# Turning k and q on VectorE for seven more units, with two homes for the rows that are turned

## The chip, the cores and the metric

The kernel runs on one core of a Trainium2 chip. The metric is the device time of one execution in microseconds (us), the median of several runs. Beside the runs there is one execution taken by the hardware profiler; its span and its own time are given below.

## The reference

An mLSTM cell is followed by a multiplicative feed-forward block. The inputs q, k, v and o_gate have shape (4, 8, 768, 40): batch, heads, positions and head dimension, in float32. The weights of the feed-forward block are float64, w1 and w2 (320, 1024), w3 (1024, 1024), w_out (1024, 320).

```python
for t in range(S):                                   # the cell
    m_new = maximum(f[t] + m, i[t])
    f_stab, i_stab = exp(f[t] + m - m_new), exp(i[t] - m_new)
    m = m_new
    C = f_stab * C + i_stab * outer(v[t], k[t])
    n = f_stab * n + i_stab * k[t]
    h = C @ q[t];  denom = max(abs(n @ q[t]), 1)
    y[t] = sigmoid(o_gate[t]) * h / denom

x = y.transpose(0, 2, 1, 3).reshape(3072, 320)       # the feed-forward block
out = ((x @ w1) * (x @ w2)) @ w3 @ w_out
```

## The kernel before

**Units and steps.** The sequence is cut into 6 chunks of 128 positions, and each chunk of each of the 4 batches is a unit: 24 units, n from 0 to 23, each with all 8 heads. A unit is again two halves of 64 positions. The main loop runs over steps s from 0 to 29. In step s the function `quarter_work` computes the inner part of unit s (the products of k and q, `ss`, and the products that go into the state, `pc`) and the outputs of unit s - 1 (`ph`, `pi`), all in one PSUM tile named `cell`. Around it the step brings in the inputs of later units, does a part of the feed-forward block on tokens that are finished, and converts a piece or two of the weights.

**Turning.** The product of k and q needs both with the head dimension on the partitions. `turn(n)` makes `kT` and `qT` for a unit. Before the change it has two ways. For units below `N_DVE` = 17, TensorE transposes k and q from `kbuf` and `qbuf` by an identity, four 128x128 transposes each into a PSUM tile `pt`, and ScalarE copies each tile to SBUF; this is issued at the beginning of step n. For units from 17 on, `load_turned(n)` brings the rows of k and q from HBM in a layout of their own, eight loads of 80 KB in place of the load of q (k is loaded in the usual way too, as the state needs it), and VectorE transposes blocks of 32x32, one instruction for k and one for q; this is issued at the end of step n - 1, behind the last instruction of the outputs. The rows lie in `gates`, a memory whose first use, the recurrence over the gates, is over after the beginning. There is one home for them, so the rows of unit n + 1 can be written when those of unit n have been turned.

**The feed-forward block.** `x_trans` turns the cell's output of units 0 to 14 on TensorE (tile `px`); for later units it goes by way of HBM (`send`, `get_back`) and VectorE (`x_turn`). `up` and `up_rest` compute x @ w1 and x @ w2 into tiles `pa` and `pb`, ScalarE copies `pa` to `a_sb`, and VectorE multiplies `pb` by it into `ab`. `w3_mm` multiplies w3 by w_out once, block by block (tile `wp`), so that `ffn_out` needs one product (tile `po`). The tiles `pt`, `px`, `wp`, `pa`, `pb` and `po` take four PSUM banks in turn.

**Words.** The float64 weights come as raw 64-bit words. `fetch` calls a piece (512 KB, a tile `raw`, four buffers), ScalarE scales its upper words, and VectorE makes float32 of it in `to_f32` (four instructions, tiles `ex`, `ma`, then the result); a piece of w3 is also transposed on VectorE (`w3T`). Two or three pieces are converted in a step, two in each of steps 9 to 15. The number of pieces that are called ahead of those converted is two in the first two steps and three afterwards.

**What sets the order.** TensorE's instructions run in the order in which they are written (`in_order`). Up to step 6 the other engines keep the written order as well (`keep_order`). Afterwards the framework's planner orders them by its own estimates, within the dependencies; it may place a conversion of a step ahead of that step's `pw`. The outputs are held behind the product `pw` (`issue_after`). All loads and the writes to HBM inside the kernel are issued by SyncE, in one queue; only the final output and three loads at the start are issued by ScalarE. Each waits there until its buffer is free, and what stands behind it waits too. In the written order a step issues the broadcast weights `pw` of unit s + 3 (`load_u`), then k, q, v and the output gate of unit s + 2 (`load`, `load_o`), then the outputs' way through HBM (`send`), the turned rows of unit s + 1 (`load_turned`), `get_back`, and at the end the raw words.

Lines of the profile: matmuls are recorded at L90, transposes on TensorE at L93; L296 is ScalarE's copy of `pt`, L288 VectorE's transposes of the turned rows, L347 the product `pw`, L351 and L356 the state, L367 to L383 the outputs, L567 the eviction to `ab`; for SyncE, L125 loads k, q and v, L134 the turned rows, L139 the output gate, L145 `pw`, L170 the raw words.

Of the kernel before, what the change touches and what calls it, by code (L numbers as in the profile page):

```python
# [8 lines left out]
FP = mybir.dt.float32  # L9
# [7 lines left out]
def kernel(  # L17
# [28 lines left out]
    B, H, S, D = q.shape  # L46
    L = 64
    P = 128
    NT = S // L
    NT2 = S // P  # L50
    NU = NT2 * B
    NP = H // 2
    DP = 64
# [11 lines left out]
    const = ctx.enter_context(tc.tile_pool(name="const", bufs=1))  # L65
# [9 lines left out]
    def mps(shape, name):  # L75
        pool = banks.pop(0)
        banks.append(pool)
        return pool.tile(shape, FP, name=name, tag="m")
# [13 lines left out]
    def transpose(out, in_, n=P):  # L92
        in_order(nc.tensor.transpose(out, in_, ident[0:n, 0:n]))  # L93
# [4 lines left out]


    NB, NBQ = 4, 3  # L100
    N_DVE = 17
    qbuf = [const.tile([P, H, DP], FP, name=f"qbuf{i}") for i in range(NBQ)]
    kbuf = [const.tile([P, H, DP], FP, name=f"kbuf{i}") for i in range(NB)]
    vbuf = [const.tile([P, H, D1], FP, name=f"vbuf{i}") for i in range(NB)]
    ident = const.tile([P, P], FP, name="ident")
# [12 lines left out]
    def rows(src, n):  # L118
        c, b = divmod(n, B)
        return src[b, :, c * P:(c + 1) * P, :].rearrange("h p d -> p h d")  # L120

    def load(n):
        for dst, src in ((kbuf[n % NB][:, :, 0:D], k), (qbuf[n % NBQ][:, :, 0:D], q), (vbuf[n % NB][:, :, 0:D], v)):
            if src is not q or n < N_DVE:
                nc.sync.dma_start(out=dst, in_=rows(src, n))  # L125

    def load_turned(n):
        c, b = divmod(n, B)
        for dst, src in zip(turned_in, (k, q)):
            for hip in range(2):  # L130
                of = src[b].rearrange("(p two) s d -> two p s d", two=2)[hip, :, c * P:(c + 1) * P, :]
                for j in range(2):
                    p0, c0 = hip * DP + j * 32, (1 - j) * 32
                    nc.sync.dma_start(out=dst[p0:p0 + 32, c0:c0 + NP * RAW].rearrange("r (p e) -> r p e", p=NP),  # L134
                                      in_=of.rearrange("p (r f) d -> r p (f d)", f=4))

    def load_o(n):
        o_t[n] = io.tile([P, H, D], FP, name="o_in", tag="o_in", bufs=4)
        nc.sync.dma_start(out=o_t[n], in_=rows(o_gate, n))  # L139

    def load_u(n):
        c, b = divmod(n, B)
        src = U_d[2 * c:2 * c + 2, b * H:(b + 1) * H, :].rearrange("x h t -> x (h t)")
        for x in range(2):
            nc.sync.dma_start(out=weights_tile(n)[halves[x]].rearrange("p h t -> p (h t)"),  # L145
                              in_=src[x:x + 1].to_broadcast([L, H * L]))
# [76 lines left out]
    def scale_next():  # L223
        scaled.append(pend.pop(0))
        scale(scaled[-1][1])
# [31 lines left out]
    qT_t, kT_t, vw_t, before_t, y_t, x_t = {}, {}, {}, {}, {}, {}  # L257

    def out_gate(n):
        nc.scalar.activation(out=o_t[n], in_=o_t[n], func=AF.Tanh, scale=0.5)  # L260
# [11 lines left out]
    def weights(n):  # L272
        c, b = divmod(n, B)
        src = weights_tile(n) if c else spread(n)
        pw = weights_tile(n)
        for h in range(H):
            nc.scalar.activation(out=pw[:, h, :], in_=src[:, h, :], func=AF.Exp, bias=aT[:, c, b * H + h:b * H + h + 1])  # L277
        for r in halves:
            nc.gpsimd.affine_select(out=pw[r], in_=pw[r], compare_op=OP.is_ge, fill=0.0, base=0,  # L279
                                    pattern=[[0, H], [1, L]], channel_multiplier=-1)  # L280

    def turn(n):


        if n >= N_DVE:
            for src, dst, name in zip(turned_in, (kT_t, qT_t), ("kT", "qT")):
                dst[n] = sb.tile([128, NP, P], FP, name=name, tag=name)
                nc.vector.transpose(out=dst[n].rearrange("i p (r f) -> i p f r", f=4),  # L288
                                    in_=src[:, 32:TB].rearrange("i (p f d) -> i p f d", p=NP, f=4)[:, :, :, 0:32])
            return  # L290
        for src, dst, name in ((kbuf[n % NB], kT_t, "kT"), (qbuf[n % NBQ], qT_t, "qT")):
            pt = mps([128, NP, P], "pt")
            for p in range(NP):
                transpose(pt[:, p, :], src[:, 2 * p:2 * p + 2, :].rearrange("p a b -> p (a b)"))
            dst[n] = sb.tile([128, NP, P], FP, name=name, tag=name)
            nc.scalar.copy(out=dst[n], in_=pt)  # L296

    def weighted(n):
        c, b = divmod(n, B)
        vw_t[n] = sb.tile([P, H, D1], FP, name="vw", tag="vw")  # L300
        nc.gpsimd.tensor_tensor(out=vw_t[n], in0=vbuf[n % NB], op=OP.mult,
                                in1=wT[:, c, b * H:(b + 1) * H].unsqueeze(2).to_broadcast([P, H, D1]))

    def decayed(new, old, n, x):
        c, b = divmod(n, B)
        nc.gpsimd.tensor_tensor(out=new, in0=old, op=OP.mult, in1=decay[:, b * NP:(b + 1) * NP, 2 * c + x:2 * c + x + 1]  # L306
                                .to_broadcast([P, NP, D1]))
# [78 lines left out]
    def send(n):  # L386


        y = y_t.pop(n)
        for cc in range(KF):  # L390
            nc.sync.dma_start(out=y_d[n][:, :, cc, :], in_=y[:, cc * P:(cc + 1) * P].rearrange("t (i c) -> t i c", c=32))
        for i in range(0, 4, 2):
            nc.sync.dma_start(out=y_d[n][:, i:i + 2, KF, :], in_=y[:, KF * P:DM].rearrange("t (i c) -> t i c", c=32))
# [16 lines left out]
    def twice(n):  # L410
        nc.gpsimd.tensor_copy(out=y_t[n][:, DM:DM + REM], in_=y_t[n][:, KF * P:DM])
# [16 lines left out]
    TB = 32 + NP * RAW  # L428
    gates = const.tile([P, 2 * TB], FP, name="gates")
    f_sb, a, F, U, on = (gates[0:RG, i * TC:(i + 1) * TC] for i in range(5))  # L430

    turned_in = [gates[:, i * TB:(i + 1) * TB] for i in range(2)]
    w, g = f_sb, on
    M = const.tile([RG, GC + 1], FP, name="M")
    dec = const.tile([RG, GC], FP, name="dec")
# [151 lines left out]
    todo = w12[KF * 2 + 1:] + [("wo", i, 0) for i in range(FO)] + [("w3", ko, part) for ko in range(FO) for part in range(2)]  # L587
# [3 lines left out]
    turned, converted, fetched = 0, 2, 2 * KF + 1  # L591

    for s in range(len(n_up)):
        if B <= s + 3 < NU:
            load_u(s + 3)
        if s + 2 < NU:
            load(s + 2)
            load_o(s + 2)
        if 0 < s < B - 1:
            weights(s + 1)  # L600
            out_gate(s)
        if s < NU:
            weighted(s)
            if s >= B:
                decayed(state[s % B][1], state[s % B][0], s, 0)
            if 0 < s < N_DVE:
                turn(s)
        if NY <= s - 2 < NU:
            send(s - 2)
        elif 0 <= s - 2 < NY:  # L610
            twice(s - 2)
        if N_DVE <= s + 1 < NU:
            load_turned(s + 1)
        if NY <= s - 2 < NU:
            get_back(s - 2)
        while turned < min(s - 2, NY):
            x_trans(turned)
            turned += 1
        fold()
        for _ in range(n_down[s]):  # L620
            ffn_out(*downs.pop(0))
        now = [ups.pop(0) for _ in range(n_up[s])]
        open_ups = [up(*x) for x in now]
        if len(now) == 1 and turned == s - 2 < NY:
            x_trans(turned)
            turned += 1

        def rest():
            for x in open_ups:
                up_rest(*x)  # L630

        gated = None
        if s <= NU:
            gated = quarter_work(s, rest)
        else:
            rest()
        with tc.issue_after(gated.ins) if gated else nullcontext():
            if NY <= s - 2 < NU:
                x_turn(s - 2)
            if N_DVE <= s + 1 < NU:  # L640
                turn(s + 1)
        if s == 0:
            gate_cols(g, gT, nc.scalar.copy)
            out_gate(0)
            scale_next()
            weights(1)
        if s == NU:
            cell_psum.close()
            banks.append(ctx.enter_context(tc.tile_pool(name="ps_x", bufs=4, space=bass.MemoryType.PSUM)))
        if B - 1 <= s < NU:  # L650
            if s + 1 < NU:
                weights(s + 1)
            out_gate(s)
        for _ in range(n_cvt[s] if s < len(n_cvt) else 0):
            convert()
            converted += 1
        while todo and fetched < converted + (2 if s < 2 else 3):
            fetch(*todo.pop(0))
            fetched += 1
        if s + 1 == pinned:  # L660
            for ins in keep_order(front):
                behind.enter_context(tc.issue_after(ins))
# [30 lines left out]
```

## Time and profile before

| what | value |
|---|---|
| median of 3 runs | 474.29 us (473.12 to 476.47) |
| profiled execution, its own time | 475.94 us |
| profiled execution, span | 474.2 us |
| TensorE matmul busy | 450.0 us (95%) |
| VectorE busy | 241.0 us (51%) |
| ScalarE busy | 142.4 us (30%) |
| GpSimd busy | 84.2 us (18%) |
| moved by DMA | 49.28 MB in 135,770 packets, mean 104 GB/s |
| granted TensorE clock, mean | 0.986 |

The span reaches from the first instruction to the last; the execution's own time is 1.74 us longer. Busy times are shares of the span over stages that differ; matmuls overlap each other, so a busy TensorE need not be at its peak. PE is TensorE, PEld its weight load, DVE VectorE, ACT ScalarE, POOL GpSimd, and SPq SyncE's queue. A line of a timeline gives the start, the duration, the engine, the source line, the operation, what is written and read, the count, and in brackets how long the engine sat idle before it and what released it. The steps concerned start, by TensorE's transposes, at 106.55 us (step 9), 119.01 (step 10), 135.78 (11), 153.51 (12), 170.29 (13), 187.06 (14), 203.83 (15), 220.60 (16) and 237.37 (17).

### The profile page before, as it was taken

What the parts mean: (1) busy time and instruction counts of PE and PEld (TensorE: products, weight loads), DVE (VectorE), ACT (ScalarE), POOL (GpSimd) and SP (SyncE); (2) the same over time, 40 slices, a digit from 0 to 9 for tenths busy, and PEclk for the clock granted to TensorE, in tenths of its full rate; (3) what the DMA queues carried; (4) which work ended last, traced back from release to release, by engine and by line L of the source; (5) the groups of instructions that cost most, each with busy time, mean ns of one, the idle gap of its engine ahead of it and who ended that gap; (6) DMA issues with size and microseconds to landing.
All of it is one profiled execution on the core that took longest, in us unless ns stands there. A gap on an engine that the chain in (4) does not pass through costs nothing.

```text
span 474.2 us, 12856 instructions
## 1 busy us (share of the span) xinstructions
PE 450.0 (95%) x5375; PEld 362.3 (76%) x5375; DVE 241.0 (51%) x501; ACT 142.4 (30%) x390; POOL 84.2 (18%) x156
## 2 busy tenths in 40 slices
PE   2867999899999999999999999999999999999997
PEld 2766878788878888788878787787877778768864
DVE  6676698988865766785351523515236043111110
ACT  3643545544243263344331212211101111011111
POOL 5341333521220222213220211100000000000000
PEclk9995999999999999999999999999999999999999
DMA  7999978599987756432452546354240220200001
GB/s 174 181 166 173 214 138 157 118 201 194 185 165 111 167 104 149 85 65 55 82 121 61 122 105 136 58 127 88 61 116 11 53 43 20 62 14 15 1 15 41
DMA packets 135770, 49.28 MB, mean 104 GB/s; under 512 B 116320, under 2 KB 126752, under 8 KB 135712
## 3 DMA queue, kind: packets, MB, share of 16 engines
q1 hardware_dynamic: 132112, 44.42, 47.8%
q10 hardware_dynamic: 3600, 4.03, 2.5%
q8 instruction: 42, 0.69, 0.6%
q14 instruction: 16, 0.13, 0.1%
HBM read 42.63 MB, written 5.80 MB: 102 GB/s over the span
## 4 chain that ended last, share of the span: by engine, by line
PE 82%; DVE 7%; issue 7%; POOL 2%; ACT 1%; DMA 0%; SPq 0%; DVEq 0%; POOLq 0%
PE pa L90 23%; PE po L90 22%; PE pb L90 16%; PE cell L90 9%; PE wp L90 7%; PE pt L93 2%; DVE h L371 1%; PE ub L90 1%; ACT pw L277 1%; PE px L93 1%; DVE o_in L381 1%; POOL state L306 1%; DVE y L383 1%; DVE h L367 1%; DVE den L378 1%
## 5 line engine op out<-in xcount | busy, mean ns | idle before, releaser
L567 DVE TENSOR_TENSOR ab<-pb,a_sb 128x512 f32<-128x512 f32 x48 | 33.1, 691 | 159.8 <-ACT a_sb L566 159.6
L90 PE MATMUL po<-w3o,ab 128*128 128x320 f32 x384 | 106.2, 435 | 0.0
L90 PEld LDWEIGHTS po<-w3o,ab 128*128 128x128 f32 x384 | 72.1, 190 | 30.1 <-issue 0.4
L90 PE MATMUL pa<-xT,w 128*128 128x256 f32 x384 | 91.1, 380 | 0.6 <-ACT xT L421 0.6
L90 PE MATMUL pb<-xT,w 128*128 128x256 f32 x384 | 90.8, 379 | 0.0
L90 PEld LDWEIGHTS pa<-xT,w 128*128 128x128 f32 x384 | 72.3, 190 | 13.3 <-ACT xT L421 1.0
L90 PEld LDWEIGHTS pb<-xT,w 128*128 128x128 f32 x384 | 72.9, 190 | 10.2 <-ACT kT L296 0.3
L566 ACT ACTIVATE a_sb<-pa 128x512 f32<-128x512 f32 x48 | 28.6, 595 | 149.4 <-PE pb L90 149.4
L90 PE MATMUL pa<-xT,wr 64*64 64x256 f32 x384 | 47.0, 383 | 0.0
L90 PE MATMUL pb<-xT,wr 64*64 64x256 f32 x384 | 47.0, 383 | 0.0
L277 ACT ACTIVATE pw<-pw,aT 128x64 f32<-128x64 f32 x160 | 40.8, 338 | 18.1 <-DMA pw<-U_d 18.1
L279 POOL TENSOR_SCALAR_AFFINE_SELECT pw<-pw 64x512 f32<-64x512 f32 x48 | 35.8, 745 | 52.5 <-ACT pw L277 51.0
L306 POOL TENSOR_TENSOR state<-state,decay 128x164 f32<-128x164 f32 x40 | 19.5, 491 | 139.7 <-issue 53.6
L90 PEld LDWEIGHTS pa<-xT,wr 64*64 64x64 f32 x384 | 25.8, 132 | 16.8 <-issue 7.8
L90 PE MATMUL wp<-wo,w3T 128*128 128x320 f32 x128 | 35.8, 432 | 0.0
L574 ACT COPY o_sb<-po 128x320 f32<-128x320 f32 x24 | 10.2, 423 | 76.6 <-PE po L90 76.4
L90 PEld LDWEIGHTS cell<-vbuf,pw 64*64 64x64 f32 x768 | 27.7, 142 | 6.2 <-issue 2.0
L90 PEld LDWEIGHTS wp<-wo,w3T 128*128 128x128 f32 x128 | 23.7, 190 | 8.9
L90 PE MATMUL cell<-vbuf,pw 64*64 64x41 f32 x768 | 27.6, 232 | 2.4 <-issue 1.4
L347 DVE TENSOR_TENSOR pw<-cell,pw 128x512 f32<-128x512 f32 x24 | 16.5, 686 | 21.7 <-PE cell L90 21.7
L90 PEld LDWEIGHTS pb<-xT,wr 64*64 64x64 f32 x384 | 25.8, 132 | 0.0
L371 DVE TENSOR_TENSOR h<-cell,h 64x328 f32<-64x328 f32 x48 | 23.8, 497 | 1.1
(88 smaller groups left out, 463.4 us busy)
## 6 DMA issues: line engine op xcount, KB each, us to landing
raw<-in_moe_w_dram SPq DMA_DIRECT2D x64, 128.0 KB, 3.2
pw<-U_d SPq DMA_DIRECT2D x40, 128.0 KB, 4.1
kbuf<-in_k_dram SPq DMA_DIRECT2D x24, 160.0 KB, 4.6
vbuf<-in_v_dram SPq DMA_DIRECT2D x24, 160.0 KB, 5.0
o_in<-in_o_gate_dram SPq DMA_DIRECT2D x24, 160.0 KB, 3.7
out_dram<-o_sb ACTq DMA_DIRECT2D x24, 160.0 KB, 2.0
raw<-in_moe_w_dram SPq DMA_DIRECT2D x7, 512.0 KB, 6.0
qbuf<-in_q_dram SPq DMA_DIRECT2D x17, 160.0 KB, 5.0
```

The costliest lines, as they stand in the source:

```text
L90: in_order(nc.tensor.matmul(out, lhsT=lhsT, rhs=rhs, start=start, stop=stop))
L93: in_order(nc.tensor.transpose(out, in_, ident[0:n, 0:n]))
L277: nc.scalar.activation(out=pw[:, h, :], in_=src[:, h, :], func=AF.Exp, bias=aT[:, c, b * H + h:b * H + h + 1])
L279: nc.gpsimd.affine_select(out=pw[r], in_=pw[r], compare_op=OP.is_ge, fill=0.0, base=0, pattern=[[0, H], [1, L]], channel_multiplier=-1)
L306: nc.gpsimd.tensor_tensor(out=new, in0=old, op=OP.mult, in1=decay[:, b * NP:(b + 1) * NP, 2 * c + x:2 * c + x + 1] .to_broadcast([P, NP, D1]))
L347: first_read = nc.vector.tensor_tensor(out=pv, in0=ss, in1=pv, op=OP.mult)
L367: nc.vector.tensor_tensor(out=h.rearrange("p (n two) d -> p two n d", two=2), in0=pi, in1=gT[:, c, hs].rearrange("p (n two) -> p two n", t ...
L371: nc.vector.tensor_tensor(out=h[r], in0=ph[x], in1=h[r], op=OP.add)
L378: nc.vector.tensor_scalar(out=den, in0=den, scalar1=1.0, scalar2=2.0, op0=OP.max, op1=OP.mult)
L566: nc.scalar.mul(out=a_sb, in_=pa, mul=UP ** -2)
L567: nc.vector.tensor_tensor(out=ab_t[gr][j][:, fs[0]:fs[-1] + 1, t0:t0 + a_sb.shape[-1]], in0=pb, in1=a_sb, op=OP.mult)
L574: nc.scalar.copy(out=o_sb, in_=po)
```

## The change

`N_DVE` goes from 17 to 10: units 10 to 16 are turned by VectorE too, so their transposes on TensorE, ScalarE's copies and the plain loads of q go, and eight loads of turned rows and two transposes on VectorE come for each. The three buffers of q become slices of one memory, `q_all`. The turned rows have two homes that take turns: even units in `gates`, odd units in `q_all`, whose q rows are no longer needed by then. `load_turned(s + 1)` is issued as the first thing of step s, ahead of the loads of the units further on. From step 9 on (the tenth step), words are called two pieces ahead of the conversions where it was three.

```diff
     NB, NBQ = 4, 3
-    N_DVE = 17
-    qbuf = [const.tile([P, H, DP], FP, name=f"qbuf{i}") for i in range(NBQ)]
+    N_DVE = 10
+    q_all = const.tile([P, NBQ * H * DP], FP, name="q_all")
+    qbuf = [q_all[:, i * H * DP:(i + 1) * H * DP].rearrange("p (h d) -> p h d", d=DP) for i in range(NBQ)]
...
     def load_turned(n):
         c, b = divmod(n, B)
-        for dst, src in zip(turned_in, (k, q)):
+        for dst, src in zip(turned_in[n % 2], (k, q)):
...
         if n >= N_DVE:
-            for src, dst, name in zip(turned_in, (kT_t, qT_t), ("kT", "qT")):
+            for src, dst, name in zip(turned_in[n % 2], (kT_t, qT_t), ("kT", "qT")):
...
-    turned_in = [gates[:, i * TB:(i + 1) * TB] for i in range(2)]
+    turned_in = [[mem[:, i * TB:(i + 1) * TB] for i in range(2)] for mem in (gates, q_all)]
...
     for s in range(len(n_up)):
+        if N_DVE <= s + 1 < NU:
+            load_turned(s + 1)
         if B <= s + 3 < NU:
             load_u(s + 3)
...
             twice(s - 2)
-        if N_DVE <= s + 1 < NU:
-            load_turned(s + 1)
         if NY <= s - 2 < NU:
             get_back(s - 2)
...
-        while todo and fetched < converted + (2 if s < 2 else 3):
+        while todo and fetched < converted + (3 if 2 <= s < 9 else 2):
             fetch(*todo.pop(0))
```

## The prediction

> **What bounds the kernel now.** I read the page's busy line and its slices first, then the chain of waits in the steps concerned, then the busy time by step, then VectorE's and SyncE's timelines in one step. Busy line, and of the slices (11.9 us each) PE, DVE and DMA:
>
> ```profile
> PE 450.0 (95%) x5375; PEld 362.3 (76%) x5375; DVE 241.0 (51%) x501; ACT 142.4 (30%) x390; POOL 84.2 (18%) x156
> ...
> PE   2867999899999999999999999999999999999997
> DVE  6676698988865766785351523515236043111110
> DMA  7999978599987756432452546354240220200001
> ```
>
> TensorE is at 9 in all slices but one from the fifth to the last but one. What leaves its queue after 93 us shortens the run, unless another engine starts to hold it. But from 118 to 225 us (the 11th to the 19th slice), where the change works, DVE stands at 5 to 8, and DMA begins there at 9 and 8: the cover is thin.
>
> The chain of waits, around the last step with the old turning (16) and the first with the new (17); columns are start, us, what:
>
> ```profile
> 220.60 1.02 PE pt L93 x8
> 221.62 0.33 PE px L93 x3
> 221.95 4.31 PE wp L90 x16
> ...
> 235.05 2.32 PE cell L90 x123
> 237.37 0.48 PE px L93 x3
> 237.85 4.31 PE wp L90 x16
> ```
>
> The eight `pt` transposes of a unit lie on the path. From the end of `cell` to the start of `wp` it is 1.35 us with them (1.02 + 0.33) and 0.48 without.
>
> Busy time by step (columns: window, length, PE, PEld, DVE, ACT, POOL, clock, DMA share, GB/s), steps 10, 11, 13 and 16:
>
> ```profile
> 119.01:135.78 16.77, 16.77 (x221) 13.81 (x221) 12.25 (x26) 5.91 (x15) 2.73 (x6) 1.00 0.98 175
> 135.78:153.51 17.73, 16.98 (x221) 13.79 (x221) 11.54 (x24) 6.75 (x20) 3.91 (x6) 1.00 0.72 138
> ...
> 170.29:187.06 16.77, 16.77 (x220) 13.81 (x221) 11.88 (x25) 6.57 (x18) 4.78 (x9) 1.00 0.71 149
> ...
> 220.60:237.37 16.77, 16.77 (x220) 13.81 (x221) 8.65 (x18) 7.71 (x24) 5.47 (x9) 1.00 0.49 95
> ```
>
> A step is 16.77 us of TensorE work without a hole; step 11 has one of 0.76 us amid its `pt` (the chain calls it "issue"). VectorE has 4 to 8 us free.
>
> VectorE's timeline: where it idles in step 13, and what a turning costs it in step 17:
>
> ```profile
> 173.28 0.33 DVE L356 TENSOR_TENSOR state<-cell,state 128x164 f32<-128x164 f32 x1 [1.45 <-POOL state L306]
> ...
> 184.56 0.69 DVE L567 TENSOR_TENSOR ab<-pb,a_sb 128x512 f32<-128x512 f32 x1 [1.76 <-ACT a_sb L566]
> 185.75 0.69 DVE L567 TENSOR_TENSOR ab<-pb,a_sb 128x512 f32<-128x512 f32 x1 [0.50 <-ACT a_sb L566]
> 187.14 0.69 DVE L347 TENSOR_TENSOR pw<-cell,pw 128x512 f32<-128x512 f32 x1 [0.70 <-PE cell L90]
> ...
> 242.35 1.12 DVE L288 STREAM_TRANSPOSE kT<-gates 128x512 f32<-128x512 f32 x1
> 243.30 1.10 DVE L288 STREAM_TRANSPOSE qT<-gates 128x512 f32<-128x512 f32 x1
> ```
>
> SyncE's timeline at steps 9 and 10:
>
> ```profile
> 116.62 1.09 SPq L145 DMA_DIRECT2D pw<-U_d  x2
> 117.75 0.59 SPq L125 DMA_DIRECT2D kbuf<-in_k_dram  x1
> 118.38 0.58 SPq L125 DMA_DIRECT2D qbuf<-in_q_dram  x1
> 119.06 2.22 SPq L125 DMA_DIRECT2D vbuf<-in_v_dram  x1
> 121.38 1.01 SPq L139 DMA_DIRECT2D o_in<-in_o_gate_dram  x1
> 122.50 5.36 SPq L170 DMA_DIRECT2D raw<-in_moe_w_dram  x8
> ```
>
> SyncE has no hole here. It comes to step 9's loads at 116.6, when TensorE has been in step 9 since 106.55: ten us late. In steps 13 and 14 it is on time (172.15 and 185.68).
>
> **What the Trainium skill says.** "TensorE: Matmul & The Clock Gate", PE-mode transpose, gives about 275 ns for a 128x128 transpose inside a kernel. The trace agrees on one (median 273), but on the path they are pipelined, 1.02 / 8 = 0.13 us each. "VectorE: DVE Perf Modes", The three transpose paths: VectorE turns blocks of 32x32 only. That is why rows must be brought in a special layout; here one 128x512 takes 1.09. "Perfetto Trace Analysis", What "DMA-bound" means, names the issuing engine's sequencer, solid with DMA slices, as a bound of its own: SyncE looks so until about 145. "DMA: Bandwidth & Descriptors", Why small descriptors are slow: each packet pays about 3 beats over its 32-byte beats. The turned rows go in packets of 640 bytes (23 beats) where plain rows have 160 (8 beats), so by that page's figures, as an estimate, the four times as many bytes of a turned load of k and q against one plain load cost 2.9 times as much. No run so far isolates it.
>
> **The change part by part.**
>
> *TensorE.* Units 10 to 16 lose eight transposes each, seven steps times 1.35 - 0.48 = 0.87: 6.1 us off the path. The bounds: nothing, if another engine holds each step at 16.77; 10.4 us, if the mean busy time of the `pt` matmuls (25.2 us over 136, 0.185 each) were paid 56 times. I take 6.1, because step 17 shows the sequence without `pt`. The hole in step 11 (17.73 - 16.77 = 0.96) lies amid the removed work, but with "issue" as its cause it may reopen elsewhere: I take half, 0.5, between 0 and 1.0.
>
> *ScalarE* loses 14 copies of 0.59 us, 8.3 us. It is 30% busy and nothing waits for it there: worth nothing. PSUM tiles per step go from eight to six, so `px` and `wp` next take the banks of the first `pa` and `pb`. `wp` then waits for the first `ab` of the step before. In step 13 that ends at 185.25 and `wp` follows 0.48 after the cell's end at 187.06: some 2 us to spare.
>
> *VectorE* gains 14 transposes of 1.09, 2.18 per step. Steps 10 to 16 hold 78.6 us of it (the windows' DVE sum); with 15.3 more, 93.9 in a stretch of 118.4 - 7.1 = 111.3, or 84%. The fullest step is the tenth: 12.25 + 2.18 = 14.43, and its wait for GpSimd's `state` (1.05) makes 15.5 against a step of 15.90. In step 13, idle was 1.45 + 1.76 + 0.50 + 0.70 = 4.41; it must now hold 2.18 more in a step 0.87 shorter, so 1.36 is left, all inside the GpSimd wait. That wait shrinks when VectorE is late (0.58 at 238.96). So it fits, with about 0.4 to 1 us. Queued behind the transposes are the word conversions and the `ab` evictions, and for `ab` waits the bank of `wp`. I charge 0.5 us in all for a late eviction, between 0 and 6.1.
>
> *SyncE and DMA.* Per unit the plain q load goes (160 KB, 0.58 us of SyncE) and eight loads of 80 KB come (0.43 each where DMA is free, 0.67 as `raw` at 122.50 where it is full: 3.4 to 5.4 us). They now stand ahead of `pw`, k, v, `o_in` and the `y` writes of their step, and all of these go out that much later. A step's issues then come to 1.09 + 0.59 + 2.2 + 1.0 + 5.4 (`raw`) + 5.4 = 15.7 at most, against 15.9. In step 9 just one piece of words is called instead of two, since the lead drops from three to two: 512 KB and 2.7 us less, against 480 KB more of rows. So SyncE begins step 9 at about 116.0, the rows of unit 10 are out by 119.5 to 121.4 and land some 2.4 us later or a little more. VectorE's `y` of that step ended at 124.55, and `kT` is first in line. That is just in time. Unit 11: out by about 134.4, due after 139. Later ones keep some 3 us.
>
> The `pw`, k and v moved back are used one to two steps on. A piece called in step s is converted in step s + 1, and its buffer (four) held a piece converted in step s - 1, so SyncE no longer waits for `ma` in the same step (16.1 us of such waits after 140). I count that as nothing, since it lies off the path.
>
> *Two homes.* The rows of n go where those of n - 2 were, turned a whole step before. The first use of the new home overwrites q of units 8 and 9, read by 107.6; SyncE comes there at about 128. In steps 17 to 23 the loads merely go earlier; TensorE has no hole there: nothing.
>
> Sum: 6.1 + 0.5 - 0.5 = 6.1 us. The profiled execution took 475.94 with a span of 474.2; it becomes 469.8 with 468.1. The median of the runs is 1.65 under the profiled one: 474.29 - 6.1 = 468.2.
>
> **The rivals.**
>
> A. VectorE becomes the bound in steps 10 to 15. For it: 15.5 of 15.9, and an order in which conversions already slip ahead of `pw` (four of them ran at 134.75 to 137.9, and `pw` 2 us late). Against: step 8 ran 11.08 in 12.46 (89%) without a hole on TensorE. At 16.5 a step the gain is 7 x 0.27 = 1.9: 472.4.
>
> B. The rows come late, the slower end. SyncE at 15.7 a step and ten us behind doesn't catch up; VectorE, in order, stands before `kT`, with the conversions and `ab` behind it. Its step is 14.5 + 0.6 + the lateness; above 16.77 the change loses, so lateness over 1.7 us in each of the seven steps decides. At 3 us: 7 x 1.3 = 9.3 slower, 483.6. Against: step 10 already drops to 175 GB/s and SyncE has recovered by step 13, with waits of its own to give up.
>
> C. The q buffers, now slices of one memory, are held as one: each turning on TensorE in steps 1 to 8 would wait for the q load just issued (5.0 us to land). 8 x 5.0 is the most; with half of it 474.3 - 6.1 + 20 = 488. Against: in `gates`, sliced likewise, VectorE's memset ran at 0.9 us while a load into another slice landed at 2.7.
>
> D. The path pays the full 10.4: 463.9.
>
> **How the numbers follow.** About 1% (469.55 to 479.03) is what a measurement of this kernel can tell from no change. Main forecast 62%: 55 below 469.55, 7 within. A 18%: 2 faster, 16 within. B 12%: 10 slower, 2 within. C 5% slower. D 3% faster. That gives 0.60, 0.25, 0.15. The main case alone runs from 466.3 (no stall, the hole gone, 0.9 us for the runs' scatter) to 470.5 (2 us of late evictions); the range 465.8 to 476 takes in A, and leaves out D, C and most of B.
>
> **What would show it.** Right: no `pt` after 109 us; 15.9 us steps from 10 to 16 with `px` (0.48) straight after `cell`; step 17 starting some 6 to 7 us before 237.4; 12 to 14.5 us of DVE a step; landing of the turned rows before `y` ends. Wrong by A: PE waiting for `ab` at `wp` or `pa`. Wrong by B: DVE idle before `kT`, released by a DMA. Wrong by C: steps 1 to 8 longer, `pt` waiting for `qbuf`.

## The result, and the profile after

The changed kernel takes 512.24 us (511.29 to 513.13, four runs) against 475.38 in the same comparison: 1.0776 times as long, 95% interval 1.0715 to 1.0837. The prediction was 468.2 with a range to 476. It was wrong in sign and size.

The profiled execution took 513.13 with a span of 511.4. Of its page, the busy line, then TensorE's slices (12.8 us each here) and its granted clock:

```profile
PE 462.5 (90%) x5319; PEld 369.4 (72%) x5319; DVE 256.1 (50%) x515; ACT 135.0 (26%) x376; POOL 85.3 (17%) x156
...
PE   3888999899699786969687999999999999999997
...
PEclk9665899999979988889897999999999999999999
```

The work moved as meant: 56 transposes fewer on TensorE (5375 instructions became 5319), 14 more on VectorE. But TensorE has 12.5 us more of busy time, not less, it falls to 6 in four slices between 128 and 256 us where it stood at 9 before, and its clock falls with it. Busy time by step in the changed kernel (steps 10 to 16, columns as before):

```profile
120.95:142.83 21.88, 16.54 (x212) 13.42 (x213) 16.77 (x31) 5.75 (x15) 4.37 (x8) 0.93 0.87 182
142.83:160.65 17.82, 17.82 (x213) 14.16 (x213) 10.38 (x20) 4.71 (x14) 2.19 (x5) 0.89 0.73 158
160.65:181.38 20.73, 16.31 (x213) 13.18 (x213) 13.44 (x25) 5.64 (x16) 4.88 (x8) 0.99 0.45 111
181.38:203.78 22.40, 17.97 (x212) 14.38 (x213) 13.42 (x25) 5.39 (x15) 3.98 (x6) 0.88 0.47 113
203.78:226.91 23.13, 18.70 (x212) 14.76 (x213) 13.42 (x25) 5.39 (x15) 3.98 (x6) 0.87 0.46 104
226.91:250.43 23.52, 19.09 (x213) 15.02 (x213) 13.43 (x25) 5.38 (x15) 3.98 (x6) 0.86 0.32 65
250.43:272.43 22.00, 17.58 (x213) 14.16 (x213) 13.42 (x25) 5.40 (x15) 3.98 (x6) 0.89 0.32 65
```

The seven steps take 151.5 us; before they took 118.4. In six of them TensorE has a hole of 4.4 or 5.3 us (length less PE busy: 21.88 - 16.54, 20.73 - 16.31 and so on), 27.5 in all. The list of waits, for TensorE after 93 us, has the same sum and names the releaser:

```profile
PE cell L90 <- DVE qT L289: 27.5, 6, 5.3
```

TensorE waits in the middle of `cell`, at the products of k and q, for VectorE's transposed q. VectorE's timeline in step 10 shows why it is late:

```profile
126.22 0.47 DVE L384 TENSOR_TENSOR y<-h,o_in 128x320 f32<-128x320 f32 x1
...
131.49 0.71 DVE L239 STREAM_TRANSPOSE w3T<-w 128x512 f32<-128x512 f32 x1
134.34 0.69 DVE L568 TENSOR_TENSOR ab<-pb,a_sb 128x512 f32<-128x512 f32 x1 [2.14 <-ACT a_sb L567]
135.21 0.69 DVE L568 TENSOR_TENSOR ab<-pb,a_sb 128x512 f32<-128x512 f32 x1 [0.17 <-ACT a_sb L567]
135.81 0.42 DVE L187 TENSOR_SCALAR ex<-raw 128x512 uint32<-128x512 uint32 x1
...
139.06 0.71 DVE L239 STREAM_TRANSPOSE w3T<-w 128x512 f32<-128x512 f32 x1
139.70 1.04 DVE L289 STREAM_TRANSPOSE kT<-gates 128x512 f32<-128x512 f32 x1
140.59 1.06 DVE L289 STREAM_TRANSPOSE qT<-gates 128x512 f32<-128x512 f32 x1
142.90 0.69 DVE L348 TENSOR_TENSOR pw<-cell,pw 128x512 f32<-128x512 f32 x1 [1.26 <-PE cell L90]
```

Between the outputs (`y`, done at 126.7) and the transposes (139.7) stand three conversions (the third is a conversion of step 10 that was moved ahead) and both evictions of the next step, one of them at the price of an idle 2.1 us. The transposes are the last thing before `pw`, which needs their result. The rows of this unit had been there long before. SyncE's timeline:

```profile
117.08 1.87 SPq L135 DMA_DIRECT2D gates<-in_k_dram  x4
118.99 1.86 SPq L135 DMA_DIRECT2D gates<-in_q_dram  x4
```

The last load goes out by 120.85, and these eight loads land 2.5 to 3.6 us after issue (median 3.1), so by about 124.5, before `y` is done. VectorE stands idle before none of the transposes of these steps, but it idles earlier in the step, for other inputs. Step 13:

```profile
185.92 0.49 DVE L384 TENSOR_TENSOR y<-h,o_in 128x320 f32<-128x320 f32 x1
188.66 0.43 DVE L187 TENSOR_SCALAR ex<-raw 128x512 uint32<-128x512 uint32 x1 [2.25 <-ACT raw L176]
...
196.20 0.69 DVE L568 TENSOR_TENSOR ab<-pb,a_sb 128x512 f32<-128x512 f32 x1 [4.45 <-ACT a_sb L567]
...
200.65 1.04 DVE L289 STREAM_TRANSPOSE kT<-q_all 128x512 f32<-128x512 f32 x1
```

The rows of this unit went out by 162.94 and landed within 3.9 us, so both transposes could have run at 186.4. VectorE idles 6.7 us for other inputs and turns the rows 14 us later. It is the order in which the planner put them.

The rest of the loss is slower work, at a lower clock. From the chain of waits, `wp` in step 11, after a hole, and in step 12, with none before it:

```profile
143.66 5.88 PE wp L90 x16
...
161.13 4.31 PE wp L90 x16
```

The same 16 matmuls take 1.6 us longer after the hole. In the seven steps TensorE is busy for 124.0 us (the column's sum). That the hole causes this is tested below.

### The profile page after: what moved, and what is told of

Its sections match the earlier page's. It is cut to its first block, busy times and chain, and to the rows that moved or that the text cites. A ratio compares the mean times of both kernels' runs of the same rounds, so it can differ in the third digit from the quotient of the medians.

```text
span 511.4 us, 12828 instructions
## 1 busy us (share of the span) xinstructions
PE 462.5 (90%) x5319; PEld 369.4 (72%) x5319; DVE 256.1 (50%) x515; ACT 135.0 (26%) x376; POOL 85.3 (17%) x156
## 4 chain that ended last, share of the span: by engine, by line
PE 71%; DVE 10%; issue 9%; DMA 4%; POOL 2%; SPq 2%; ACT 1%; DVEq 0%; POOLq 0%; ACTq 0%
PE po L90 21%; PE pa L90 20%; PE pb L90 14%; PE wp L90 8%; PE cell L90 6%; DMA raw<-in_moe_w_dram 2%; DMA w3o<-in_moe_w_dram 2%; PE px L93 1%; DVE kT L289 1%; DVE qT L289 1%; DVE h L372 1%; POOL pw L280 1%; DVE ma L188 1%; DVE ex L187 1%; SPq L126 1%
## 5 line engine op out<-in xcount | busy, mean ns | idle before, releaser
L90 PE MATMUL pa<-xT,w 128*128 128x256 f32 x384 | 92.9, 386 | 0.6 <-ACT xT L422 0.6
L90 PEld LDWEIGHTS pa<-xT,w 128*128 128x128 f32 x384 | 73.4, 193 | 13.7 <-ACT xT L422 1.0
L307 POOL TENSOR_TENSOR state<-state,decay 128x164 f32<-128x164 f32 x40 | 21.0, 529 | 171.8 <-PE cell L90 79.4
L90 PE MATMUL cell<-qT,kT 40*64 40x64 f32 x768 | 22.1, 257 | 29.3 <-DVE qT L289 27.5
L280 POOL TENSOR_SCALAR_AFFINE_SELECT pw<-pw 64x512 f32<-64x512 f32 x48 | 35.8, 745 | 60.2 <-ACT pw L278 58.5
L90 PE MATMUL wp<-wo,w3T 128*128 128x320 f32 x128 | 45.0, 516 | 0.0
L90 PEld LDWEIGHTS cell<-qT,kT 40*64 40x64 f32 x768 | 18.3, 162 | 30.4 <-DVE qT L289 28.2
L90 PEld LDWEIGHTS wp<-wo,w3T 128*128 128x128 f32 x128 | 29.6, 238 | 12.8 <-issue 6.5
L575 ACT COPY o_sb<-po 128x320 f32<-128x320 f32 x24 | 10.2, 426 | 101.2 <-PE po L90 101.2
```

Of the source, the lines that this page charges most:

```text
L90: in_order(nc.tensor.matmul(out, lhsT=lhsT, rhs=rhs, start=start, stop=stop))
L575: nc.scalar.copy(out=o_sb, in_=po)
```

## The experiments

Three theories. 1: the order, as read above. 2: the rows land late (rival B). 3: VectorE has no room for 2.1 us more a step (rival A). Ratios are to the kernel before on the same chip.

**The transposes held in front.**

```diff
         def rest():
-            for x in open_ups:
-                up_rest(*x)
+            with after_turn(s):
+                for x in open_ups:
+                    up_rest(*x)
...
         for _ in range(n_cvt[s] if s < len(n_cvt) else 0):
-            convert()
+            with after_turn(s + 1):
+                convert()
```

`after_turn(n)` holds what VectorE does inside it behind the transposes of unit n.

> The changed kernel, with VectorE's order held by hand in steps 9 to 15: the two transposes of the turned rows come straight after the outputs, the word conversions of the step and the next step's ab evictions behind them. Nothing else differs. Theory 1 (order: the rows are there, but the planner put the transposes behind both conversions and both evictions, so that TensorE waits for qT in the middle of cell): no wait of PE for qT, steps 10 to 16 near 15.9 us, 467 to 470 in all. Theory 2 (the rows land late, rival B of the prediction): VectorE stands before kT, released by a DMA, with all else behind it; 500 or more. Theory 3 (VectorE has no room for the 2.1 us): steps of 17 us or more, 478 to 490.

525.24 us, ratio 1.1037 (1.0941 to 1.1133): slower than the change itself. Theories 1 and 3 miss. The number lies in the range of theory 2 (500 or more), but not by its mechanism: VectorE starts `kT` at 125.42, straight behind `y`, and waits for no rows. The wait for `qT` is gone and another has its place. TensorE's timeline in step 11 of this run:

```profile
135.79 0.55 PE L93 MATMUL px<-ident,y 128*128 128x128 f32 x3
143.19 7.09 PE L90 MATMUL wp<-wo,w3T 128*128 128x320 f32 x16 [6.85 <-DVE den L382]
```

`wp` waits 6.9 us. The name `den` is of what ran at the same moment; what `wp` reads is `w3T`, and VectorE's timeline has its second half finished at 143.04. With the transposes held in front, the planner put the conversions behind the evictions, where VectorE idled 5.7 us for `a_sb`, and the second conversion in among the next outputs. So theory 2 is out for this step; theories 1 and 3 were still open, for this run moved the order fault instead of removing it.

**The loads at their old place.** `load_turned(s + 1)` goes back behind the outputs' writes.

> The changed kernel, with the loads of the turned rows issued where they were before, behind the loads of the units further on and the writes of the outputs. Here the planner puts both conversions ahead of the evictions and the transposes behind them, so nothing but the two transposes (2.1 us) stands between the last eviction and the products of k and q. Theory 1 (order): TensorE waits some 2.2 us a step instead of 5.4, and keeps more of its clock: 480 to 490. Theory 2 (late rows): the loads go out later than in the changed kernel, so it is slower than 512. Theory 3 (no room): the same VectorE work as in the changed kernel, about 512.

488.48, ratio 1.0255 (1.0156 to 1.0355), and TensorE waits 12.8 us for `qT`, six times, instead of 27.5. Theory 1 had 480 to 490; theory 2 wanted it slower than the change, theory 3 about the same. Later loads made it 24 us faster: in steps 12 to 16 the planner now puts both conversions ahead of the evictions, and the wait is 1.5 us a step. In step 10 it still leaves a conversion between the evictions and the transposes, and there the wait is 5.3 as before.

**Three pieces ahead to the end.** The last hunk of the change undone.

> The changed kernel, with words called three pieces ahead to the end, as before. Theory 1 (order): the transposes stand last in VectorE's order in nearly all of steps 9 to 14 as well, so 503 to 514. If the shorter lead were the cause (words arrive late, conversions late, transposes behind them): well below, 475 or less. Theory 2 (late rows): one more piece of words ahead of the rows in SyncE's queue, so at or above 512.

512.06, ratio 1.075 (1.0649 to 1.0851), with 27.5 us of waits for `qT`. The shorter lead is not the cause. Between theories 1 and 2 this run doesn't decide, as it fits both.

**All but the seven units.** `N_DVE` back to 17, the rest of the change kept. In this run the second home is written while q rows are still wanted there, so a part of q is replaced by other rows; the work is the same.

> The changed kernel, with VectorE turning from unit 17 on as before; what remains of the change is the two homes, q as slices of one memory, the earlier place of the loads and the shorter lead of the words. Theory 1 (order) and theory 3: 473 to 477, since no transposes fall in steps 9 to 15. If the one memory or the shorter lead costs time by itself (rival C): longer steps 1 to 8 or 9 to 15, above 480.

478.13, ratio 1.0013 (0.9972 to 1.0054); 1.1 us more than expected, but no change against the kernel before. The one memory for q, the place of the loads and the lead cost nothing that shows, and rival C falls.

**The whole order held.** Beside the transposes, `pw` is held behind the evictions, the evictions behind both conversions, and ScalarE's `a_sb` behind its scaling of the words:

```diff
-            first_read = nc.vector.tensor_tensor(out=pv, in0=ss, in1=pv, op=OP.mult)
+            with tc.issue_after(done_ab[0].ins) if N_DVE <= n <= 16 else nullcontext():
+                first_read = nc.vector.tensor_tensor(out=pv, in0=ss, in1=pv, op=OP.mult)
...
         def rest():
-            for x in open_ups:
-                up_rest(*x)
+            with ExitStack() as es:
+                if N_DVE <= s <= 16:
+                    for ins in done.values():
+                        es.enter_context(tc.issue_after(ins.ins))
+                for x in open_ups:
+                    up_rest(*x)
...
-            convert()
+            with after_turn(s + 1):
+                convert()
```

`done` holds VectorE's last conversion and ScalarE's last scaling, `done_ab` the last eviction.

> The changed kernel, with VectorE's order of steps 9 to 15 held throughout: outputs, the two transposes of the turned rows, both conversions, the two evictions of the next step, then the product pw; ScalarE scales the words ahead of the next step's a_sb. The run pinned held only the transposes, and the planner pushed the conversions behind the evictions and in among the next outputs, where wp then waited for w3T. Theory 1 (order alone; the DMAs are in time and VectorE has room): no wait of PE for qT or w3T, steps 10 to 16 near 15.9 us, 467 to 471. Theory 2 (rows or words land late): VectorE stands before kT or ex, released by a DMA or by ScalarE's scaling, and the evictions behind it are late: 480 or more. Theory 3 (no room): VectorE without idle time, wp or pb waiting for ab: 475 to 485.

470.6, ratio 0.9869 (0.9827 to 0.9911), as theory 1 had it: 1.3% faster than the kernel before. Same instructions and loads as in the changed kernel, 42 us less. VectorE waits for no load between 93 and 250 us, so theory 2 is out for all these steps. Busy time by step, the first three and the last of the seven:

```profile
123.37:139.27 15.90, 15.90 (x213) 12.96 (x213) 13.22 (x26) 4.93 (x13) 2.89 (x7) 1.00 0.88 176
139.27:155.17 15.90, 15.90 (x213) 12.96 (x213) 13.09 (x25) 5.68 (x19) 3.16 (x7) 1.00 0.81 178
155.17:171.07 15.90, 15.90 (x212) 12.96 (x213) 13.06 (x25) 4.18 (x10) 3.13 (x7) 1.00 0.84 199
...
218.76:234.66 15.90, 15.90 (x212) 12.96 (x213) 12.94 (x26) 5.51 (x15) 3.17 (x7) 1.00 0.45 92
```

Seven steps of 15.90 us, 111.3 in all, with no hole and the full clock. VectorE's timeline, step 11:

```profile
142.10 0.33 DVE L363 TENSOR_TENSOR state<-cell,state 128x164 f32<-128x164 f32 x1 [1.82 <-POOL state L312]
...
145.08 0.49 DVE L390 TENSOR_TENSOR y<-h,o_in 128x320 f32<-128x320 f32 x1
145.49 1.14 DVE L294 STREAM_TRANSPOSE kT<-q_all 128x512 f32<-128x512 f32 x1
146.48 1.07 DVE L294 STREAM_TRANSPOSE qT<-q_all 128x512 f32<-128x512 f32 x1
...
152.73 0.71 DVE L239 STREAM_TRANSPOSE w3T<-w 128x512 f32<-128x512 f32 x1
153.47 1.32 DVE L574 TENSOR_TENSOR ab<-pb,a_sb 128x512 f32<-128x512 f32 x2
155.25 0.69 DVE L354 TENSOR_TENSOR pw<-cell,pw 128x512 f32<-128x512 f32 x1 [0.46 <-PE cell L90]
```

After a wait of 1.8 us for GpSimd's `state`, the rest of the step's VectorE work runs without a break, and it is done half a microsecond before `pw` can start. There is room, and just so much.

**The same, with the transposes last.** In steps 10 to 16 the two transposes stand behind the evictions. Work and loads are those of the run before, but two parts of the order differ, and the expectation counts only the first: the conversions, held behind the transposes there, are held behind nothing here.

> The kernel of the run full with one thing different: the two transposes stand behind the two evictions of their step (from step 10 to 16) instead of ahead of the conversions. Same instructions, same loads. Theory 1 (order): TensorE waits some 2.2 us a step in the middle of cell, 7 x 2.2 = 15 more than full, with a little of the clock lost: 482 to 488. Theories 2 and 3: as slow or as fast as full, since neither the loads nor the amount of work differ.

490.57, ratio 1.0301 (1.023 to 1.0371): 20.0 us above the held order. TensorE waits 14.5 us for `qT`: 5.3 in step 10, where the planner put a third conversion between the evictions and the transposes (135.96 to 139.91), then 1.5 each time. The other 5.5 lie elsewhere, in good part in `wp`, which takes 5.68 us once and 6.16 twice in place of 4.47 (in a timeline; the chain of waits gives the same undisturbed matmuls 4.31). A bit more than expected, and by the order alone, since work and loads are the same; but the wait in step 10 is by the place of the conversion too.

**What a wait costs beside its length.** The transposes, last again, are done three times over; then TensorE is given something to do meanwhile.

> The kernel of the run late with each of the transposes of steps 10 to 16 done three times over, the same result written each time: 4.2 us more between the last eviction and the products of k and q. TensorE should wait some 6.3 us a step. If the wait alone counts: 7 x 6.3 = 44 above full, 510 to 514. If TensorE's clock also falls with the wait, as the granted clock of the changed kernel suggests: 1.5 to 2 us more a step for px and wp, 520 to 528.

527.97, ratio 1.1086 (1.1016 to 1.1156). TensorE waits 44.8 us in seven steps (9.8 in step 10, with the third conversion in front again, then 5.1 to 6.0), and the run is 57.4 longer than the held order: 12.6 us, or 1.8 a step, beyond the wait. The two profiles alone give 13.7: from 117.54 to 287.30, by the starts of `px`, the seven steps take 58.5 more than the 111.3 of `full`.

> The kernel of the run late3, in which TensorE does 22 matmuls of no use (128x256, into the part of cell that the products of k and q then overwrite) while it would wait, some 4.8 us of work a step. If only the length of the wait counts: as slow as late3 or slower. If the idle time costs clock: wp back at 4.3 us, and 8 to 12 us faster than late3, though TensorE has more to do. The planner may also place conversions behind the transposes here, which would shorten the wait a little.

537.92, ratio 1.1295 (1.1224 to 1.1366). The filling was twice as long as I had sized it (9.8 us a step: `cell` takes 12.15 in place of 2.32), so the total says little. But no wait above 0.3 us was left, and `wp` took 4.31 throughout.

> The run late3_fill again with half the filling: there the 22 matmuls took 9.8 us of a step and not 4.8, more than the wait that they were to fill. With 11 of them TensorE works 4.9 us of a wait of 6.3. If only the length of the wait counts: as slow as late3, 528. If the idle time costs clock: wp at 4.3 us and 513 to 519.

517.26, ratio 1.0851 (1.0767 to 1.0934): 10.7 us faster than `late3`, though TensorE does some 34 us more (half of 9.8, seven times). Waits fell from 44.8 to 10.2 us, so filling and waiting together are as long as before; what is gone is the slow stretch after the wait. TensorE's timelines after a wait of 5.1 us in `late3`, and after one of 0.3 with the filling:

```profile
165.91 1.13 PE L90 MATMUL cell<-qT,kT 40*64 40x64 f32 x32 [5.14 <-DVE qT L295]
166.98 0.90 PE L93 MATMUL px<-ident,y 128*128 128x128 f32 x3
167.67 5.97 PE L90 MATMUL wp<-wo,w3T 128*128 128x320 f32 x16
```

```profile
170.56 0.69 PE L90 MATMUL cell<-qT,kT 40*64 40x64 f32 x32 [0.34 <-DVE qT L295]
171.19 0.55 PE L93 MATMUL px<-ident,y 128*128 128x128 f32 x3
171.57 4.47 PE L90 MATMUL wp<-wo,w3T 128*128 128x320 f32 x16
```

Each line is longer after the wait: 1.13 against 0.69, 0.90 against 0.55, 5.97 against 4.47. The filled run holds both cases: its one long wait, 4.9 us in step 10, is followed by a `wp` of 5.34, its six of 0.3 to 1.2 us by 4.47 each time.

**Which parts of the change are needed, once the order is held.** The loads at their old place and three pieces ahead, with the order of `full`.

> The kernel of the run full with two parts of the change undone: the turned rows are called at their old place, behind the loads of the units further on, and words three pieces ahead to the end. What remains is the turning by VectorE, the two homes and the held order. If order is all that matters, 468 to 473, the same as full. If the earlier place and the shorter lead are needed for the rows of unit 10 and 11 to be in time (SyncE is ten us late there): a wait of VectorE before kT in steps 9 to 11 and 474 to 482.

467.58, ratio 0.9795 (0.9755 to 0.9835), the lowest median of this study. Steps 10 to 16 are 15.90 here too. VectorE now waits 7.2 us in all before `kT` and `qT`, released by the rows' loads, and TensorE doesn't feel it. So neither the earlier place nor the shorter lead is needed for the gain. Whether they cost anything against this run isn't settled: the intervals overlap, and the profiles differ ahead of the changed steps (step 10 begins at 123.37 in `full`, at 120.11 here), which these parts reach only in step 9.

**Two units more**, from unit 8 on.

> The kernel of the run full with VectorE turning from unit 8 on, so also in steps 7 and 8, where three pieces of words are converted. There VectorE has some 11.1 us of work before the change and 13.3 with the transposes, in steps that TensorE could do in 11.6. Theory 3 holds here: steps 8 and 9 take about 13 us or more instead of 12.4, wp or pb wait for ab, and the total is 471 to 476, no faster than full. If VectorE's room is not the limit even here: two units more at 0.87, 468 to 470.

476.05, ratio 1.0001 (0.9973 to 1.0029): the whole gain is gone again. VectorE runs almost without a break from 87 to 122 us, and step 9 takes 19.0 us instead of 12.5:

```profile
101.91:120.90 18.99, 12.34 (x198) 10.05 (x198) 17.57 (x33) 7.35 (x18) 6.04 (x9) 0.93 0.92 199
```

17.6 us of VectorE work in front of `wp`, which waits 6.0 us for `w3T`. Here theory 3 holds: where three pieces are converted in a step there is no room, with the order held in this way.

**The rows called a step earlier**, with no order held.

> The changed kernel without any held order, but with the rows of unit s + 2 called in step s, a step earlier (behind that step's other loads; the home is free by then). The planner now puts the transposes straight behind the outputs in all but one of steps 9 to 15, so it was its estimate of the rows' landing that put them last. But it puts the end of the second conversion behind pw, as in the run pinned. Theory 1 (order): no or little wait for qT, but wp waits for w3T some 4 to 6 us a step: 495 to 520. If the late rows were the cause by themselves: 467 to 475.

523.53, ratio 1.0982 (1.0928 to 1.1036). The transposes now come straight behind the outputs in most steps (`y` at 125.29, `kT` at 125.70 in step 10), no wait for `qT` is left, and `wp` waits instead, 35.5 us (29.1 put down to `w3T`, 6.4 to `den` at the same moment). So the moment at which the rows are called decides the transposes' place. Most likely the planner takes the rows to be there later than they are: in the changed kernel they landed before `y` was done and were turned last all the same. Its estimates themselves can't be seen in a profile, so this is not shown, and how far off they are stays open.

## Why the prediction was wrong

**The step that failed** is the VectorE paragraph, with the SyncE paragraph's "`kT` is first in line". I read the place of the transposes from step 17, where they follow `y`, and counted with it in steps 10 to 16. Step 17 has no conversions; the others have two. I knew from the profile before that the planner moves conversions (rival A's "four of them" at 134.75 to 137.9 are the instructions of one conversion, five in number, ahead of `pw`), but treated VectorE's work as an amount that fits or doesn't, 15.5 of 15.9. The amount did fit, as `full` shows. What I had not asked is what stands last ahead of the point where TensorE needs it. The term mis-sized is "0.5 us in all for a late eviction, between 0 and 6.1": in its place stand 27.5 us of waits and 12.7 of slower work.

**The sum as it came out**, against 118.4 us for the seven steps before: less 7.1 (to 111.3, as `full` has it), plus 27.5 of waits, plus 12.7 of slower work (124.0 busy against 111.3), plus 2.1 in what follows, where `wp` of step 17 comes after the last wait (238.97 from there to the end, against 236.84 in `full`). That is 35.2 of the 37.2 by which the span grew. The other 2 us lie ahead of step 10 (120.95 against 119.01). They are there before the change does anything in that stretch: `px` of step 8 begins at 96.59, before at 94.66, and at 93.26 to 99.02 in the profiles of `late3` and `full`. I take them for scatter.

**What held.** The 0.87 us a step: 15.90 exactly, once the order is held, and the hole of step 11 gone entirely (I took half). With the order held the medians are 6.5 us apart (477.05 and 470.6), where I had forecast 6.1; so the saving was sized rightly, and the condition for getting it was missing. The cost of the changed SyncE queue: rows of unit 10 out by 120.85, inside the 119.5 to 121.4 of the prediction; they landed 3.1 us later where I had some 2.4, and still in time. Rival C was rightly small. One label was wrong: the step of 11.08 us of VectorE work in 12.46, named step 8 against rival A, is step 9 of the list (106.55 to 119.01).

**The rivals.** None of them named this. A had the right engine and the wrong quantity: too much work, with TensorE waiting for `ab`; the runs show enough room and a wait for `qT`. B had the right place of the damage, VectorE's queue ahead of the products, and a wait in each step, but by late rows; its own sign, VectorE idle before `kT` and released by a DMA, is absent. Both also took a wait for as long as it is: B's 9.3 us had no term for the clock, which came to 46% on top of the waits (12.7 on 27.5).

## What to carry to other kernels

When work moves to an engine with idle time, its place in that engine's order must be found, not just its room: ask what the planner may put between the input's arrival and the point where another engine waits, and don't read that place from a stretch where the competing work is absent. If the order matters, hold all of it; bringing one instruction to the front, by a hold (`pinned`) or by earlier loads (`early`), sent another to the back, at 523 to 525 us. And price a hole in TensorE above its length.

## What the runs showed of the hardware

A wait of TensorE of 4.4 us or more cost more than its length here. In the changed kernel a wait of 4.4 us ended at 180.5; from 182 on the granted clock was 0.81 for 6 us, and 1.00 after that. The stages (columns as before):

```profile
182.00:188.00 6.00, 6.00 (x20) 4.21 (x20) 3.61 (x11) 1.22 (x4) 1.36 (x3) 0.81 0.81 172
188.00:196.00 8.00, 8.00 (x61) 6.51 (x63) 2.95 (x5) 1.06 (x3) 0.00 (x0) 1.00 0.36 85
```

The Trainium skill, "TensorE: Matmul & The Clock Gate", Why this matters for your kernels, warns of idle gaps above some 3 us. The measured waits agree: 1.8 us lost per wait in `late3`, whose waits were 5.1 to 9.8 us. But in the run `late` some waits of 1.5 us were followed by a slow `wp` as well (6.16 us after 1.52, while it kept 4.47 after 1.53 one step earlier), so a short wait isn't always followed by full speed. Between wait and `wp` the matmuls of `cell` and `px` kept their length there (0.69 and 0.55), unlike after the long waits, so that the short wait is the cause is not shown.
